# Start of a fused attention and GLU kernel: one reciprocal earlier, half a copy on VectorE, two transposes one group later

## The chip, the cores and the metric

The kernel runs on one core of one Trainium2 chip. The metric is the device time of one execution in microseconds. An execution's span in its profile is about 2 us shorter than its time (228.0 against 229.98 in the profiled run of before).

The profile's single records, one for each instruction, give starts and ends to a nanosecond; they differ by up to 0.005 us from one view to another. A landing is the moment at which a DMA's data has arrived. An eviction is the copy of a finished group of products out of its PSUM tile (q_sb<-q_ps of 128x256 took 0.39 us in the mean in the profile of before).

## The reference, cut to what matters

```python
xn = _layernorm(A_x)                      # 2048 rows of 512, bf16
s  = _A_ref(xn, A_wqkv, A_wo)             # qkv projection, attention over 8 keys with dilation 2, 32 heads of 16
g  = silu(_B_ref(xn, w_gate, w_up, w_down))   # gelu(xn w_gate) * (xn w_up), then w_down
return A_x + s * g
```

## The kernel before

The 2048 rows are 16 tiles of 128 rows. Tiles 0 to 3 form the first block of 512. To start TensorE early, the first q and k projections are done for tiles 0 and 1 alone (256 columns), and later for tiles 2 and 3. Before it has anything to do, TensorE runs products on constants ("warm-up"). Products of 128 columns start 0.107 us apart up to 6.13 us in the profile of before and 0.056 apart from there on. That the warm-up brings this step forward is an assumption.

```python
def first_moments(t):
    nc.vector.bn_stats(out=stats[:, t, :], in_=x_sb[:, t, :])
    nc.vector.bn_aggr(out=mv[:, t, :], in_=stats[:, t, :])
    nc.scalar.activation(out=std[:, t, :], in_=mv[:, t, 1:2], func=AF.Sqrt, bias=epsc[:], scale=1.0)

def first_normalize(t):
    nc.vector.reciprocal(out=rstd[:, t, :], in_=std[:, t, :])
    normalize(t)                       # xn = (x - mean) * rstd, VectorE

def transpose(t, parts=1, copy=None):
    tr = mm.tile([P, NC * P], BF16, name="tr", tag="mm")
    # ... four TensorE transposes into tr, then tr -> xnT in `parts` pieces:
    for k in range(parts):
        c = slice(k * NC // parts, (k + 1) * NC // parts)
        if copy is None:
            nc.scalar.activation(out=dst[:, c], in_=src[:, c], func=AF.Copy)
        else:
            copy(out=dst[:, c], in_=src[:, c])

# ... the start
warm_up(18, TQ // 2); warm_up(4, P)
first_moments(0); first_moments(1)
first_normalize(0); transpose(0)
first_normalize(1); warm_up(4, P)
transpose(1, parts=2); warm_up(4, P)
first_moments(2); first_moments(3)
first_normalize(2); first_normalize(3)
# ... q of tiles 0 and 1: 16 products into q_ps, chunks 0 and 1 of xnT first
for fo in range(NC):
    qkv(0, fo, 0, HQ, qs[fo])          # ScalarE evicts the four q groups
transpose(HT, copy=nc.vector.tensor_copy)              # tile 2
for fo in range(NC, 2 * NC):
    qkv(0, fo, 0, HQ)                  # k groups: 4 products, ScalarE evicts
    if fo == NC:
        transpose(HT + 1, copy=nc.vector.tensor_copy)  # tile 3
```

The warm-up results, the transposes and the k groups all take their PSUM space from one pool, `mm`, of four banks (`mm = pool("mm", 4, space=PSUM)`); q_ps has its own. I call the k groups k0 to k3 and the transposes of tile n tr*n*.

The softmax here doesn't subtract the row's maximum and nothing guards it: scores larger than these inputs give would overflow.

## Time and profile before

| | before |
|---|---|
| time, median of 3 runs | 229.72 us (229.64 to 230.14) |
| span of the profiled execution | 228.0 us |
| TensorE busy | 222.4 us, 98% |
| VectorE busy | 147.6 us, 65% |
| ScalarE busy | 129.8 us, 57%, 213 instructions |
| q_ps starts | 6.88 us |
| TensorE's clock reaches full rate | 6.13 us |

TensorE is busy throughout (98%), so only what delays its products counts. The page's sum says nothing on a change in the first 11 us: for that the chain of work and the timelines of these microseconds are to be read, which the prediction shows. The row on the clock is read from single product records: the starts of 128-column products lie 0.107 us apart before it and 0.056 apart after it.

### The profile page before, as it was taken

Reading aid. Unit: us, or ns where it says so; the run is one execution under the profiler, and the core shown is the slowest. Engines: PE = TensorE matmul, PEld = TensorE weight load, DVE = VectorE, ACT = ScalarE, POOL = GpSimd, SP = SyncE. Lnnn points to the kernel's source line nnn. Section 1 sums busy time; section 2 is a strip of 40 time slices with the busy share of each in tenths; the row PEclk is TensorE's granted clock in tenths of the full one; section 3 lists DMA queues with packets and bytes.
Section 4 is the critical chain, followed back from the end, with each engine's and each line's share of the span. In section 5 each row is a group of like instructions: output and inputs, shape, how many; then the busy total and the mean of one; then the engine's idle time right before and its main releaser. Section 6 shows DMA issues by size and latency. Waiting matters only on the chain.

```text
span 228.0 us, 3495 instructions
## 1 busy us (share of the span) xinstructions
PE 222.4 (98%) x1300; PEld 106.8 (47%) x1320; DVE 147.6 (65%) x234; ACT 129.8 (57%) x213; POOL 12.8 (6%) x44
## 2 busy tenths in 40 slices
PE   8999999999999999999999999999999999999993
PEld 6864444444444444444444444444444444444453
DVE  4585996999496298865945369735476429943324
ACT  3779769774423876467621686746642387647210
POOL 1046023100000000110000000000000000000000
PEclk9999999999999999999999999999999999999999
DMA  6999589971399211110287511110149700001011
GB/s 166 354 372 372 146 169 197 247 202 38 101 195 206 70 25 29 26 29 0 92 169 168 139 30 23 26 35 5 39 119 206 169 27 3 0 6 26 0 45 48
DMA packets 31264, 24.62 MB, mean 108 GB/s; under 512 B 10896, under 2 KB 31248, under 8 KB 31248
## 3 DMA queue, kind: packets, MB, share of 16 engines
q1 hardware_dynamic: 31248, 24.41, 42.8%
q8 instruction: 10, 0.16, 0.3%
q14 instruction: 6, 0.05, 0.1%
HBM read 18.74 MB, written 4.34 MB: 101 GB/s over the span
## 4 chain that ended last, share of the span: by engine, by line
PE 95%; ACT 2%; issue 1%; DVE 0%; ACTq 0%; DVEq 0%
PE u_ps L238 21%; PE y_ps L394 21%; PE g_ps L238 19%; PE qkv_ps L238 17%; PE s_ps L410 6%; PE L_ps L295 3%; PE o_ps L357 3%; PE warm_ps L220 2%; PE q_ps L238 1%; ACT u L384 1%; ACT L382 1%; PE tr L203 1%; PE den_ps L315 0%; ACT xnT L212 0%; ACT ge L382 0%
## 5 line engine op out<-in xcount | busy, mean ns | idle before, releaser
L238 PE MATMUL u_ps<-xnT,wu_sb 128*128 128x512 bf16 x224 | 57.5, 379 | 0.3
L238 PE MATMUL g_ps<-xnT,wg_sb 128*128 128x512 bf16 x213 | 56.3, 379 | 0.4
L394 PE MATMUL y_ps<-wd_sb,h 128*128 128x512 bf16 (+1 forms) x236 | 50.2, 366 | 0.1
L386 DVE TENSOR_TENSOR h<-ge,u 128x512 bf16<-128x512 bf16 x56 | 23.7, 424 | 37.0 <-ACT u L384 36.6
L284 DVE TENSOR_TENSOR pk<-q_sb,k_sb 128x2048 bf16<-128x2048 bf16 x32 | 37.5, 1216 | 7.0 <-ACT k_sb L259 7.0
L382 ACT ACTIVATE ge<-g_ps 128x512 bf16<-128x512 f32 x56 | 33.5, 598 | 14.9 <-PE g_ps L238 13.8
L384 ACT ACTIVATE u<-u_ps 128x512 bf16<-128x512 f32 x56 | 33.5, 598 | 14.7 <-PE u_ps L238 14.7
L238 PE MATMUL qkv_ps<-xnT,wqkv_sb 128*128 128x512 bf16 (+1 forms) x203 | 40.5, 354 | 0.3
L343 DVE TENSOR_TENSOR pv<-E,v_arr 128x2048 bf16<-128x2048 bf16 x32 | 38.6, 1218 | 0.2 <-issue 0.2
L394 PEld LDWEIGHTS <-h 128*128 128x128 bf16 x238 | 23.3, 98 | 25.3
L238 PEld LDWEIGHTS <-wu_sb 128*128 128x128 bf16 x224 | 21.9, 98 | 26.6 <-issue 0.3
L238 PEld LDWEIGHTS <-wg_sb 128*128 128x128 bf16 x224 | 21.3, 98 | 27.3 <-issue 3.0
L402 ACT ACTIVATE sl<-y_ps 128x512 bf16<-128x512 f32 (+1 forms) x17 | 9.7, 572 | 41.4 <-PE y_ps L394 39.0
L238 PEld LDWEIGHTS <-wqkv_sb 128*128 128x128 bf16 x224 | 21.8, 98 | 19.8 <-issue 0.4
L418 DVE TENSOR_TENSOR m<-s_ps,sl 128x512 bf16<-128x512 f32 (+1 forms) x17 | 11.2, 657 | 22.2 <-PE s_ps L410 22.2
L410 PE MATMUL s_ps<-wo_sb,oT 128*128 128x512 bf16 (+1 forms) x66 | 15.8, 366 | 0.2
L262 ACT ACTIVATE vst<-qkv_ps 128x512 bf16<-128x512 f32 x16 | 9.6, 598 | 6.5 <-PE qkv_ps L238 6.5
L188 POOL TENSOR_TENSOR rstd<-rstd,mhalf 128x1 f32<-128x1 f32 x12 | 7.7, 640 | 87.4 <-DVE rstd L185 87.4
L259 ACT ACTIVATE k_sb<-qkv_ps 128x512 bf16<-128x512 f32 (+1 forms) x20 | 10.2, 516 | 3.5 <-PE qkv_ps L238 3.2
L369 DVE TENSOR_TENSOR oT<-o_ps,rb 128x1024 bf16<-128x1024 f32 x8 | 9.4, 1216 | 3.1 <-DMA rb<-rs_d 3.1
L256 ACT ACTIVATE q_sb<-qkv_ps 128x512 bf16<-128x512 f32 (+1 forms) x16 | 8.7, 544 | 3.2 <-PE qkv_ps L238 3.0
L410 PEld LDWEIGHTS <-oT 128*128 128x128 bf16 x68 | 6.7, 98 | 7.2
(46 smaller groups left out, 105.9 us busy)
## 6 DMA issues: line engine op xcount, KB each, us to landing
v_arr<-vT SPq DMA_DIRECT2D x16, 520.0 KB, 5.4
vT<-vst SPq DMA_DIRECT2D x16, 128.0 KB, 1.8
out_dram<-o_t SPq DMA_DIRECT2D x15, 128.0 KB, 1.8
wg_sb<-in_B_w_gate_dram SPq DMA_DIRECT2D x2, 896.0 KB, 10.7
wu_sb<-in_B_w_up_dram SPq DMA_DIRECT2D x2, 896.0 KB, 12.3
wd_sb<-in_B_w_down_dram SPq DMA_DIRECT2D x1, 1792.0 KB, 12.3
wqkv_sb<-in_A_wqkv_dram SPq DMA_DIRECT2D x3, 512.0 KB, 5.2
x_sb<-in_A_x_dram SPq DMA_DIRECT2D x3, 512.0 KB, 11.6
```

The costliest lines, as they stand in the source:

```text
L238: nc.tensor.matmul(ps, lhsT=w[:, dk, lo : lo + P], rhs=xnT[j][:, dk, i0 : i0 + n], start=(dk == 0), stop=(dk == NC - 1),)
L259: nc.scalar.activation(out=k_sb[:, c, lo : lo + n], in_=ps, func=AF.Copy)
L262: nc.scalar.activation(out=vst[:], in_=ps, func=AF.Copy)
L284: nc.vector.tensor_tensor(out=pk[:], in0=st[j]["q"][:], in1=k_sb[:, :, off : off + TQ], op=ALU.mult)
L343: nc.vector.tensor_tensor(out=pv[:], in0=st[j]["E"][:, wh, :].unsqueeze(1).to_broadcast([P, 4, TQ]), in1=st[j]["va"][:, 4 * g : 4 * g + 4, ...
L382: nc.scalar.activation(out=ge[:], in_=g_ps[:], func=AF.Gelu_apprx_tanh)
L384: nc.scalar.activation(out=u[:], in_=u_ps[:], func=AF.Copy)
L386: nc.vector.tensor_tensor(out=h[:], in0=ge[:], in1=u[:], op=ALU.mult)
L394: nc.tensor.matmul(y[:], lhsT=st[j][fc][:, tt * P : (tt + 1) * P], rhs=wd_sb[:, fc, cols], start=(fc == 0), stop=(fc == NF - 1),)
L402: nc.scalar.activation(out=sl[:], in_=y[:], func=AF.Silu)
L410: nc.tensor.matmul(s[:], lhsT=st[j]["oT"][:, g, tt * P : (tt + 1) * P], rhs=wo_sb[:, g, cols], start=(g == 0), stop=(g == NC - 1),)
L418: nc.vector.tensor_tensor(out=m[:], in0=s[:], in1=sl[:], op=ALU.mult)
```

## The change

Three things: the reciprocal of tile 0 is put between the statistics and the aggregate of tile 1, where VectorE waits anyway (0.034 us in the profile of before, 4.362 to 4.396). VectorE copies the first half of tile 1's transpose, where ScalarE copied both halves one after the other (from 6.44 and 6.72 us in before). And the transposes of tiles 2 and 3 come one k group later, since VectorE gets to these tiles later. The intent is to start q_ps earlier.

```diff
+    def first_stats(t):
+        nc.vector.bn_stats(out=stats[:, t, :], in_=x_sb[:, t, :])
     def first_moments(t):
-        nc.vector.bn_stats(out=stats[:, t, :], in_=x_sb[:, t, :])
         nc.vector.bn_aggr(out=mv[:, t, :], in_=stats[:, t, :])
 ...
-    def first_normalize(t):
+    def first_rstd(t):
         nc.vector.reciprocal(out=rstd[:, t, :], in_=std[:, t, :])
-        normalize(t)
 ...
-            if copy is None:
+            if copy is None or k % 2:
                 nc.scalar.activation(out=dst[:, c], in_=src[:, c], func=AF.Copy)
 ...
+    first_stats(0)
     first_moments(0)
+    first_stats(1)
+    first_rstd(0)
     first_moments(1)
-    first_normalize(0)
+    normalize(0)
     transpose(0)
-    first_normalize(1)
+    first_rstd(1)
+    normalize(1)
     warm_up(4, P)
-    transpose(1, parts=2)
+    transpose(1, parts=2, copy=nc.vector.tensor_copy)
     warm_up(4, P)
 ... (tiles 2 and 3: the same calls, split into their parts)
-    transpose(HT, copy=nc.vector.tensor_copy)
     for fo in range(NC, 2 * NC):
         qkv(0, fo, 0, HQ)
-        if fo == NC:
-            transpose(HT + 1, copy=nc.vector.tensor_copy)
+        if fo < NC + 2:
+            transpose(HT + fo - NC, copy=nc.vector.tensor_copy)
```

More of the change, by code (lines that the diff above doesn't have):

```diff
@@ L474 @@
     warm_up(4, P)
+    first_stats(0)
     first_moments(0)
+    first_stats(1)
+    first_rstd(0)
     first_moments(1)
-    first_normalize(0)
+    normalize(0)
     transpose(0)
-    first_normalize(1)
+    first_rstd(1)
+    normalize(1)
     warm_up(4, P)
-    transpose(1, parts=2)
+    transpose(1, parts=2, copy=nc.vector.tensor_copy)
     warm_up(4, P)
-    first_moments(2)
-    first_moments(3)
-    first_normalize(2)
-    first_normalize(3)
+    for t in (2, 3):
+        first_stats(t)
+        first_moments(t)
+    for t in (2, 3):
+        first_rstd(t)
+        normalize(t)
     q4 = att.tile([P, NC, TQ], F32, name="q4_ps", tag="quad")
```

## The prediction

> **What bounds the kernel now.** I read the page's chain of work that ended last first. It is TensorE nearly everywhere, so a microsecond is won or lost only where TensorE issues later or earlier.
>
> ```profile
> PE 95%; ACT 2%; issue 1%; DVE 0%; ACTq 0%; DVEq 0%
> ```
>
> The change touches only the first 11 us, so I read the same chain there in order of time:
>
> ```profile
> 0.84 4.43 PE warm_ps L220 x22
> 5.26 0.47 PE tr L203 x4
> 5.73 0.43 PE warm_ps L220 x4
> 6.16 0.26 PE tr L203 x4
> 6.42 0.02 issue
> 6.44 0.39 ACT xnT L212
> 6.83 0.04 issue
> 6.88 1.91 PE q_ps L238 x16
> 8.79 0.22 PE tr L203 x4
> 9.01 0.44 PE qkv_ps L238 x4
> ```
>
> The columns are start, us, what. Up to 6.42 the path runs through TensorE's own warm-up products, not through VectorE. Then ScalarE's copy of the first half of tile 1's transpose (6.44 to 6.83) holds q_ps, which starts at 6.88. From there TensorE issues without a gap, a 128x256 product each 0.109 us (16 in 1.744 us from 6.882 to 8.627, single records). The waits of TensorE and its weight load over the first 8 us agree: only two matter.
>
> ```profile
> PE q_ps L238 <- ACT xnT L212: 0.2, 1, 0.2
> PEld L238 <- DMA wqkv_sb<-in_A_wqkv_dram: 0.2, 1, 0.2
> ```
>
> The second is the q weights: their last packet lands at 6.607 and the weight load starts at 6.651. So q_ps can't start before about 6.66: at most 0.22 us is to be had. VectorE's timeline of 4 to 7 us, with start and duration:
>
> ```profile
> 4.39 0.18 DVE L173 BATCH_NORM_AGGREGATE mv<-stats 128x2 f32<-128x6 f32 x1
> 4.49 0.13 DVE L179 RECIPROCAL rstd<-std 128x1 f32<-128x1 f32 x1
> 4.66 0.41 DVE L194 TENSOR_SCALAR xn<-x_sb,mv,rstd 128x512 bf16<-128x512 bf16 x1
> 4.99 0.15 DVE L179 RECIPROCAL rstd<-std 128x1 f32<-128x1 f32 x1
> 5.18 0.41 DVE L194 TENSOR_SCALAR xn<-x_sb,mv,rstd 128x512 bf16<-128x512 bf16 x1
> ```
>
> Tile 0's normalize waits 0.17 us for the reciprocal just ahead of it. The rows that decide my prediction are ScalarE's evictions of 8.6 to 11.3 us:
>
> ```profile
> 8.82 1.21 ACT L256 ACTIVATE q_sb<-q_ps 128x256 bf16<-128x256 f32 x4 [0.59 <-PE q_ps L238]
> 9.90 1.50 ACT L259 ACTIVATE k_sb<-qkv_ps 128x256 bf16<-128x256 f32 x4
> ```
>
> All four q evictions wait for the last q_ps product (8.517 + 0.273 = 8.790). They issue 0.27 us apart, so the first k group is evicted only from 9.900 to 10.315, though TensorE finished it at 9.45.
>
> [...]
> - [...]128-column products start 0.107 us apart up to 6.064 and 0.056 apart from 6.134.[...]
> - [...]For the 128x512 bf16 copy[...] the trace has 0.424.[...] ScalarE's half copy took 0.384.
> - [...]
> - [...]Here four buffers rotate, and the change alters which group gets which.
>
> **The change, part by part.**
>
> 1. Reciprocal of tile 0 ahead of tile 1's aggregate. The aggregate must wait for its statistics (ends 4.362, starts 4.396). The reciprocal's input is ready (ScalarE's root ends at 4.179), so it goes into that gap at about 4.28. The normalize then starts about 0.10 after the aggregate, as the reciprocal does now: 4.50 in place of 4.66, ending at 4.91. But TensorE is in warm-up until 4.955 + 0.107 = 5.062, so the transposes of tile 0 move from 5.132 to 5.062, 0.07 and not 0.17. The four then issue 0.107 apart and end their block at 5.49 instead of 5.53 (0.04 won). Four warm-ups and four transposes of tile 1 follow with half of the saving lost if the clock step stays at 6.08: tile 1's transposes end at 6.38 to 6.41 (now 6.190 + 0.219 = 6.409). Gain 0.00 to 0.04, I take 0.025.
>
> 2. Half copy on VectorE. It starts 0.04 after the transposes, 6.42,[...] and q_ps starts 0.05 later: 6.76 in place of 6.88. ScalarE's half, if it waits for VectorE's, ends near 7.14; it is first needed by the ninth product at 6.76 + 0.87 = 7.63. Nothing lost there. Parts 1 and 2 together: 0.12 us gained, q_ps products issued by 8.50 (were 8.627), last one done at 8.67 (was 8.79).
>
> 3. Statistics of tile 2 now sit behind the half copy. The statistics start near 6.65 and those of tile 3 near 7.45 (was 6.994): some 0.42 us later down the line. Tile 2 is normalized by about 8.83 (now 8.40) and tile 3 by 9.34.
>
> 4. Transposes one group later, which part 3 needs. Order before: tr2, k0, tr3, k1, k2, k3. After: k0, tr2, k1, tr3, k2, k3. TensorE's work is the same (group 0.436, four transposes 0.223), and k0's weights land at 8.423, just ahead of 8.50. The buffers are not the same. The pool of four hands them out in turn. Before, k2 takes tr2's buffer, free when VectorE's copy ends at 9.475; k2 starts at 9.947 without waiting, and k3 takes k0's, free at 10.315, with its start at 10.383: 0.07 to spare. (In the records k2's first product waits on VectorE's semaphore and k3's on ScalarE's, which confirms the rotation.) After, k2 is the fourth allocation behind k0 and takes **k0's** buffer. TensorE would be ready for it at 8.50 + 2 x 0.436 + 2 x 0.223 = 9.82. But k0's eviction stands behind four q evictions: they start at 8.70, k0's at 8.70 + 1.07 = 9.77, it ends at 9.77 + 0.415 = 10.19, and the product starts 0.05 later, 10.24. So TensorE waits 0.42 us, a wait that doesn't exist now.
>
> Sum: k2 starts at 10.24 against 9.947: 0.29 us later. That is 0.42 of new wait less 0.12 of earlier start (the same work lies between). The later groups don't wait again: k3 needs tr2's buffer (VectorE has copied it by 9.8), the next q group k1's (evicted by 10.46, wanted at 11.1).
>
> **What becomes of 0.29 us.** After 10 us I looked for waits at a fixed time that could absorb it. The gap between starts of TensorE's products shows single gaps of 0.2 us, half of them missing records, and only one early wait for another engine, 21.01, on ScalarE (eviction of v, table load, gelu). That chain starts when TensorE finishes v, and moves with it. x rows 4 to 7 land at 12.136 and are transposed only at 17.77, with the normalize done at 16.6; the up weights land at 17.43 and are used at 18.85. No load is late, so nothing absorbs the shift: span 228.0 + 0.3, time 229.72 + 0.29 = 230.0.
>
> **The rivals.**
> - A. The change does what its author wants: q_ps 0.12 to 0.2 us earlier and nothing behind it, 229.55. For it: all TensorE work is equal and the wait above is inferred from the order of allocation. Against it: the semaphores in the records fit the rotation at every one of four groups.
> - B. The first part gains nothing (clock step or the 6.607 landing moves): the wait for k0's buffer counts from q_ps's end, so k2 comes at 10.34, 0.39 later, 230.1. For it: the weight load already waits for this DMA.
> - C. VectorE is late: tile 2's normalize ends at 8.9 or more and tile 2's transposes (due 8.94) wait, and ScalarE's q evictions stand behind tile 3's root. For it: only 0.05 to spare. Against it: up to 0.4 us hides under the same wait for k0's buffer. If the root came 0.2 late, 230.2.
> - D. The step of the array's clock comes at another time in other executions: either sign, some tenths, in both kernels alike. It widens the range only.
>
> **Range and chances.** The central sum is +0.29 (+0.13%), 230.0. The rivals span 229.5 to 230.2, and the three runs of before span 0.5 us. So 229.55 to 230.4 should hold it 8 times in 10. 2% is 4.6 us, over ten times any of these terms: faster or slower by over 2% would need a cause outside the first 11 us, 0.5% each.
>
> **What would show it.** Right: q_ps starts near 6.76 behind a VectorE copy of 128x256[...], ScalarE's half after it; tile 0's normalize at 4.50; the third k group starts near 10.24 after a TensorE idle of about 0.4 us, put down to ScalarE's k_sb eviction; from 11 us on all stages 0.2 to 0.4 later. Wrong: no idle at about 9.8 (then the buffers turn otherwise, rival A); q_ps not before 6.85 (B); idle ahead of tile 2's transposes of over 0.4 us (C); stages after 20 us not shifted like those at 11 us (something absorbs it).

One term of the sum goes with them: how long VectorE's half copy takes. With it parts 1 and 2 came to q_ps at 6.76 in place of 6.88, 0.12 us gained, and the sum to k2 at 10.24 against 9.947, +0.29 us, 230.0 in all. The profile of after has 0.291 us for this copy. That ScalarE's half comes after VectorE's was an assumption (in the profile of after it starts at 6.376, VectorE's ends at 6.342).

## The result, and the profile after

The changed kernel took 230.02 us (median of 6, 229.78 to 230.32), the kernel before 229.73 us in the same rounds (median of 6). The ratio is 1.0012, 95% interval 0.9999 to 1.0024: the same within 2%. The predicted number, 230.0, is met almost exactly. The profile shows at once that it isn't met for the predicted reason.

First the chain of work after, in order of time (start, us, what):

```profile
2.18 4.31 DMA wqkv_sb<-in_A_wqkv_dram
6.49 0.04 issue
6.54 1.92 PE q_ps L239 x16
8.46 0.56 PE qkv_ps L239 x4
9.02 0.22 PE tr L204 x4
9.24 0.44 PE qkv_ps L239 x4
9.68 0.22 PE tr L204 x4
9.90 7.85 PE qkv_ps L239 x56
```

q_ps starts at 6.54, not at the predicted 6.76 nor at the old 6.88, and what releases it is the landing of the q weights, no longer ScalarE's copy. k0 takes 0.56 in place of 0.44, because the k weights land at 8.37 and hold it for 0.11 us. And from the transposes of tile 3 on TensorE runs through: the predicted wait of 0.42 us ahead of k2 isn't there. (This chain counts a step from the modelled end of the one before, hence 9.90; by the single records k2's first product starts at 9.76.)

VectorE's timeline after shows that part 1 did on VectorE what was predicted, and that the half copy takes 0.29 us:

```profile
4.29 0.14 DVE L181 RECIPROCAL rstd<-std 128x1 f32<-128x1 f32 x1
4.41 0.18 DVE L175 BATCH_NORM_AGGREGATE mv<-stats 128x2 f32<-128x6 f32 x1
4.50 0.38 DVE L195 TENSOR_SCALAR xn<-x_sb,mv,rstd 128x512 bf16<-128x512 bf16 x1
4.95 0.16 DVE L181 RECIPROCAL rstd<-std 128x1 f32<-128x1 f32 x1
5.15 0.41 DVE L195 TENSOR_SCALAR xn<-x_sb,mv,rstd 128x512 bf16<-128x512 bf16 x1
6.05 0.29 DVE L215 COPY xnT<-tr 128x256 bf16<-128x256 bf16 x1 [0.49 <-PE tr L204]
```

Tile 0's normalize is at 4.50 (4.66 before), but tile 1's only at 5.15 (5.18): 0.16 us for the first, 0.03 for the second.

ScalarE's evictions keep their shape. k0 is still evicted only behind the four q evictions, but nobody waits for it:

```profile
8.50 1.21 ACT L257 ACTIVATE q_sb<-q_ps 128x256 bf16<-128x256 f32 x4 [0.21 <-PE q_ps L239]
9.57 1.64 ACT L260 ACTIVATE k_sb<-qkv_ps 128x256 bf16<-128x256 f32 x4
```

Two things must be kept apart before the traces are compared. The clock's step to full rate fell at 3.70 us in this execution and at 6.13 us in the profiled one of before. Between the two times 128-column products start 0.056 us apart here and 0.107 apart there. The step also moves without the change: two profiles of the kernel before have it at 6.13 and 5.34. So the 0.34 us by which q_ps is earlier here can't be credited to it, and neither can the 0.14 us by which the span is shorter (227.86 against 228.0). And a longer median time goes with a shorter span in the one profile. That asked for more executions of both kernels and for each part by itself.

**Theories before the experiments.** A: the buffers turn otherwise than predicted, nothing is lost, the early part gains 0.05 to 0.2 us, and the +0.29 us between the medians is scatter. B: a loss of some 0.3 us is real, and the first profile hid it behind its early clock step. C to G came up on the way and are stated where they were tested.

The built programs say which PSUM bank each tile got, so the first part of A can be looked up (tiles in the order of the program, with the number of the bank):

```
            tr2  k0   tr3  k1   k2         k3         q0 (tiles 2,3)  q1
before       1    2    3    0    1 (tr2's)  2 (k0's)   3 (tr3's)       0 (k1's)
            k0   tr2  k1   tr3  k2         k3         q0              q1
after        1    2    3    0    2 (tr2's)  1 (k0's)   3 (k1's)        0 (tr3's)
```

The pool isn't a ring. In the changed kernel k2 takes tr2's bank, which VectorE's copy frees early (at 9.70 us in the profile of after), and not k0's. With k0 in bank 1 and k2 in bank 2 the predicted wait can't come about.

### The profile page after: what moved, and what is told of

It is laid out like the page before. It is cut to its first block, busy times and chain, and to the rows that moved or that the text cites. A ratio compares the mean times of both kernels' runs of the same rounds, so it can differ in the third digit from the quotient of the medians.

```text
span 227.9 us, 3516 instructions
## 1 busy us (share of the span) xinstructions
PE 222.8 (98%) x1320; PEld 106.0 (47%) x1320; DVE 147.8 (65%) x235; ACT 129.6 (57%) x212; POOL 12.8 (6%) x44
## 4 chain that ended last, share of the span: by engine, by line
PE 94%; DMA 2%; ACT 1%; SPq 1%; DVE 0%; issue 0%; DVEq 0%
PE y_ps L395 21%; PE u_ps L239 21%; PE g_ps L239 21%; PE qkv_ps L239 18%; PE s_ps L411 6%; PE L_ps L296 3%; PE o_ps L358 3%; DMA wqkv_sb<-in_A_wqkv_dram 2%; PE q_ps L239 1%; ACT L383 1%; SPq L85 1%; PE den_ps L316 0%; ACT ge L383 0%; ACT vst L263 0%; ACT xnT L213 0%; PE tr L204 0%
## 5 line engine op out<-in xcount | busy, mean ns | idle before, releaser
L239 PE MATMUL g_ps<-xnT,wg_sb 128*128 128x512 bf16 x224 | 57.6, 379 | 0.0
```

The costliest lines, as they stand in the source:

```text
L239: nc.tensor.matmul(ps, lhsT=w[:, dk, lo : lo + P], rhs=xnT[j][:, dk, i0 : i0 + n], start=(dk == 0), stop=(dk == NC - 1),)
```

## The experiments

All outputs are right. One table first; "us" are medians of six runs, except that before has eleven:

| run | edit | us | before, same rounds | ratio, 95% interval |
|---|---|---|---|---|
| after_again | the changed kernel | 230.09 | 230.01 | 1.0000 (0.9984 to 1.0016) |
| before_again | the kernel before | 229.91 | 230.01 | 0.9991 (0.9974 to 1.0008) |
| shared_buffer | changed, k2 forced into k0's bank | 230.66 | 230.01 | 1.0025 (1.0007 to 1.0043) |
| no_shift | changed, transposes in their old place | 230.50 | 230.01 | 1.0018 (1.0001 to 1.0035) |
| recip_only | before, reciprocal alone | 229.88 | 229.95 | 0.9986 (0.9970 to 1.0002) |
| half_only | before, half copy alone | 230.02 | 229.95 | 0.9999 (0.9983 to 1.0014) |
| shift_only | before, later transposes alone | 229.88 | 229.95 | 0.9991 (0.9976 to 1.0007) |
| early_weights | changed, q and k weights loaded earlier | 230.60 | 229.95 | 1.0026 (1.0008 to 1.0043) |
| absorbed_wait | changed, ScalarE's wait taken earlier | 230.16 | 230.08 | 0.9999 (0.9978 to 1.0019) |
| absorbed_q_first | the same, q weights earlier | 230.66 | 230.08 | 1.0016 (0.9999 to 1.0034) |
| recip_again | recip_only once more | 229.94 | 230.08 | 0.9990 (0.9975 to 1.0006) |
| absorbed_padded | absorbed_wait, one idle ScalarE instruction | 230.14 | 229.80 | 1.0019 (1.0005 to 1.0033) |

The intervals are 0.13% to 0.2% wide to either side, 0.3 to 0.45 us. The terms in question are 0.02 to 0.4 us. So most verdicts rest on the single records of the traces, which repeat to some nanoseconds:

| run | clock step | x rows of tile 0 landed to tile 0's, tile 1's normalize | end of tr1 to q_ps | k2 after q_ps | first gate product to end of span |
|---|---|---|---|---|---|
| before | 6.13 | 1.812, 2.332 | 0.473 | 3.065 | 210.010 |
| before_again | 5.34 | 1.812, 2.333 | 0.472 | 3.064 | 209.996 |
| recip_again | 3.72 | 1.647, 2.290 | 0.472 | 3.078 | 210.014 |
| shift_only | 5.42 | (row landing late) | 0.473 | 3.082 | 209.997 |
| half_only | 4.38 | 1.813, 2.334 | 0.475 | 3.346 | 210.051 |
| after | 3.70 | 1.644, 2.288 | 0.525 (q weights late) | 3.218 | 210.055 |
| after_again | 3.77 | 1.643, 2.288 | 0.474 | 3.082 | 210.062 |
| no_shift | 4.38 | 1.650, 2.293 | 0.476 | 3.931 | 210.051 |
| shared_buffer | 5.14 | 1.645, 2.291 | 0.476 | 3.483 | 210.041 |
| early_weights | 6.20 | 1.645, 2.287 | 0.475 | 3.648 | 210.061 |
| absorbed_wait | 6.42 | 1.645, 2.287 | 0.379 | 3.917 | 210.058 |
| absorbed_q_first | 4.60 | 1.643, 2.288 | 0.381 | 3.254 | 210.049 |
| absorbed_padded | 6.93 | 1.645, 2.350 | 0.383 | 3.081 | 210.010 |

All are microseconds. "After q_ps" counts from q_ps's first product to k2's.

### after_again and before_again

No edit.

> The changed kernel once more, unedited, to see whether +0.29 us is real and where the step of the array's clock falls. Theory A (the third k group takes another buffer than predicted, nothing is lost, the early part gains 0.05 to 0.2 us, and +0.29 us of the medians is scatter): ratio 0.9990 to 1.0005; third k group starts 9.7 to 9.85 us. Theory B (a loss of about 0.3 us is real and the first profile happened to hide it behind an early clock step at 3.6 us): ratio 1.0008 to 1.0020, and with a clock step near 6 us a TensorE wait of 0.2 us or more between 8 and 11 us.

> The kernel before, unedited: what two sets of runs of one and the same program differ by. Ratio 1.0000, within 0.0008 either way, under both theories. If its clock step comes earlier than the 6.08 us of the first profile, q_ps starts at 6.60 to 6.70 in place of 6.88 (then the q weights' landing holds it); if it comes again near 6 us, 6.85 to 6.9.

The ratio of the changed kernel is 1.0000 this time; that of the unchanged kernel to itself is 0.9991. The kernel before had medians of 229.73, 230.01, 229.95, 230.08 and 229.80 us in five sessions, and the changed kernel 230.02 and 230.09. So +0.29 us is no more than what sessions of one kernel differ by (0.35 us; they ran on at least three chips). Within the rounds of one session the fairer measure is the ratio: 1.0012 the first time, 1.0000 the second, and 0.9991 for a kernel against itself. In after_again's profile k2 starts at 9.65 us, just before the 9.7 to 9.85 that was expected for theory A; the clock step had come at 3.77. Its first profile wasn't a lucky one that hid a loss, since the second shows no wait of 0.2 us between 8 and 11 us either. Theory B falls as far as a loss of 0.3 us goes; the interval of after_again leaves 0.16%, 0.37 us, to either side, and the sign of the difference stays open by times alone.

Before_again had its clock step at 5.34 us, and q_ps started at 6.66 in place of 6.88 with the same program. That is more than the change can do. The expected 6.60 to 6.70 came, but not for the reason given: the q weights had landed at 6.35, and ScalarE's copy still held q_ps.

### shared_buffer: the predicted wait made on purpose

```diff
+    kps = mm.tile([P, HQ], F32, name="qkv_ps", tag="mm")[:]
     for fo in range(NC, 2 * NC):
-        qkv(0, fo, 0, HQ)
+        if fo in (NC, NC + 2):                      # k0 and k2 share one tile
+            project(kps, wqkv_sb, fo * P, 0, 0, HQ)
+            qkv(0, fo, 0, HQ, kps)
+        else:
+            qkv(0, fo, 0, HQ)
```

> The changed kernel with the third k group forced into the first k group's buffer, as the prediction had supposed. Theory A: here, and not in the changed kernel, TensorE waits 0.28 to 0.42 us for ScalarE's eviction of the first k group, and the third k group starts about 10.0 to 10.25 us; ratio to the kernel before 1.0004 to 1.0016, and 1.0012 to 1.0018 times that of the changed kernel. Theory B with the buffer as the cause: the same time as the changed kernel within 0.0005.

From TensorE's and ScalarE's timelines of 8 to 12 us of this run:

```profile
9.46 0.39 PE L204 MATMUL tr<-ident,xn 128*128 128x128 bf16 x4
10.10 2.13 PE L239 MATMUL qkv_ps<-xnT,wqkv_sb 128*128 128x256 bf16 x18 [0.26 <-ACT k_sb L260]
```

```profile
8.56 1.21 ACT L257 ACTIVATE q_sb<-q_ps 128x256 bf16<-128x256 f32 x4
9.64 0.69 ACT L260 ACTIVATE k_sb<-qkv_ps 128x256 bf16<-128x256 f32 x2
```

k2 starts at 10.108, 0.419 us later than TensorE could issue it. (The 0.26 in the line is less, because the profile counts idle from the modelled end of the product before, not from its issue.) The prediction's sum for this wait was 0.42. So its arithmetic was right for a kernel in which k2 has k0's bank, and the changed kernel isn't that kernel. The median is 0.57 us above after_again of the same rounds, more than the wait; the ratio of 1.0025 lies above the expected 1.0004 to 1.0016, which its interval takes in down to 1.0007.

### recip_only and recip_again: part 1 alone

```diff
+    first_stats(0)
     first_moments(0)
+    first_stats(1)
+    first_rstd(0)
     first_moments(1)
-    first_normalize(0)
+    normalize(0)
```

> The kernel before with the reciprocal of tile 0 put ahead of tile 1's aggregate, and nothing else. Tile 0's normalize starts at 4.50 in place of 4.66. Theory A: gain 0.00 to 0.05 us at q_ps with a late clock step, up to 0.15 us with an early one, the q weights' landing (6.5 to 6.65) setting the floor; ratio 0.9993 to 1.0003. Theory B with this part as the cause: 1.0008 or more.

> The reciprocal alone once more, since the profile of its first run fell in an execution of 1343 us. Against the kernel before, counted from the landing of tile 0's rows: tile 0's normalize starts 0.16 to 0.2 us earlier, tile 1's at most 0.05 us earlier, since it waits for ScalarE's root of tile 1 and that is no earlier; so q_ps 0.0 to 0.05 us earlier. Ratio 0.9985 to 1.0007. Rival (the whole 0.17 us arrives): q_ps 0.15 us earlier.

The profiled execution of recip_only took 1343.46 us. TensorE was slow from its first to its last product; the page's lines for the span and for one tile say it:

```profile
span 1341.7 us, 3515 instructions
...
L395 PE MATMUL y_ps<-wd_sb,h 128*128 128x512 bf16 (+1 forms) x238 | 300.9, 1628 | 0.0
```

The mean of such a product was 1628 ns against 366 in the page of before, while its other five runs took 229.58 to 229.91 us. It tells nothing on the change, and the kernel was run once more.

In recip_again tile 0's normalize starts 1.647 us after its rows have landed, against 1.812: 0.165 us earlier, as predicted. Tile 1's starts 0.043 us earlier (2.290 against 2.333), and this is what q_ps hangs on. The chain is: aggregate of tile 1, root on ScalarE, reciprocal, normalize. VectorE's timelines, first before_again, then recip_again:

```profile
4.53 0.18 DVE L173 BATCH_NORM_AGGREGATE mv<-stats 128x2 f32<-128x6 f32 x1
4.62 0.13 DVE L179 RECIPROCAL rstd<-std 128x1 f32<-128x1 f32 x1
4.79 0.41 DVE L194 TENSOR_SCALAR xn<-x_sb,mv,rstd 128x512 bf16<-128x512 bf16 x1
5.12 0.16 DVE L179 RECIPROCAL rstd<-std 128x1 f32<-128x1 f32 x1
```

```profile
4.45 0.18 DVE L175 BATCH_NORM_AGGREGATE mv<-stats 128x2 f32<-128x6 f32 x1
4.55 0.38 DVE L195 TENSOR_SCALAR xn<-x_sb,mv,rstd 128x512 bf16<-128x512 bf16 x1
4.99 0.16 DVE L181 RECIPROCAL rstd<-std 128x1 f32<-128x1 f32 x1
```

In the first, the second reciprocal starts 0.33 us after the normalize. In the second the same 0.33 would put it at 4.88 (an estimate), but it waits for ScalarE's root, which ends at 4.961 in the single records, 0.51 us after the aggregate's start, as in the profile of before (4.39 to 4.90). So of 0.165 us 0.043 is left. The times of both runs lie below 1 (0.9986 and 0.9990), both with intervals that hold 1.

### half_only: part 2 alone

```diff
-            if copy is None:
+            if copy is None or k % 2:
 ...
-    transpose(1, parts=2)
+    transpose(1, parts=2, copy=nc.vector.tensor_copy)
```

> The kernel before with half of tile 1's copy on VectorE, and nothing else. VectorE's half takes 0.29 us in place of ScalarE's 0.38; here it stands in program order ahead of tile 2's statistics, so tile 2's normalize moves from 8.4 to about 8.8 and TensorE waits for it at 8.5 (transposes in their old place). Theory A: q_ps 0.1 us earlier, then a wait of 0.1 to 0.4 us at tile 2's transposes; ratio 0.9998 to 1.0012. Theory B with this part as the cause: 1.0010 or more.

The expected wait came: 0.27 us at tile 2's transposes, which VectorE's later statistics hold up (k2 comes 3.346 us after q_ps in place of 3.065). The expected gain didn't come at all: from the end of tr1 to q_ps it is 0.475 us, and 0.472 or 0.473 where ScalarE copies both halves. VectorE's copy is 0.093 us shorter (0.291 against 0.384), and q_ps starts 0.146 us after its end where it starts 0.051 after ScalarE's. The gain is used up to the last few nanoseconds. VectorE's and TensorE's lines:

```profile
6.16 0.29 DVE L214 COPY xnT<-tr 128x256 bf16<-128x256 bf16 x1 [0.49 <-PE tr L203]
```

```profile
6.59 0.60 PE L238 MATMUL q_ps<-xnT,wqkv_sb 128*128 128x256 bf16 x4 [0.24 <-DMA wqkv_sb<-in_A_wqkv_dram]
```

The DMA named in the second had landed at 6.49; the next run shows what held q_ps.

### absorbed_wait: why the half copy gains nothing

In the changed kernel the first q product has to wait for two engines: for ScalarE's copy of tile 0 and for VectorE's half of tile 1. In the built program ScalarE's wait is on the product, the DMA's on the weight load ahead of it, and VectorE's is an instruction of its own ahead of that load. Theory D is that this second wait, not VectorE, costs the time: the weight load can't be done ahead any more. The edit lets the last warm-up product read tile 0's copy, so that TensorE has waited for ScalarE by then (the helper got an argument for it):

```diff
-    warm_up(4, P)
+    warm_up(4, P, last=xnT[0][:, 0, 0:P])     # rhs of the last of the four products
```

> The changed kernel, where the last warm-up product reads tile 0's transposed copy, so that TensorE has waited for ScalarE before it comes to q_ps and has only VectorE left to wait for. Theory D (in the changed kernel VectorE's copy is 0.093 us shorter, 0.291 against 0.384, but q_ps starts 0.146 us after its end in place of 0.051, because the second wait sits on the weight load as a separate instruction; so the half copy gains nothing): from the end of VectorE's copy to q_ps 0.05 us, and from the end of tile 1's transposes to q_ps 0.38 us in place of 0.47, unless the q weights land later than that. Rival E (VectorE's writes are seen later than ScalarE's whatever waits): still 0.14 and 0.47 us. Time: at most 0.1 us less than the changed kernel, ratio to before 0.9988 to 1.0008, not to be told from it.

From the end of VectorE's copy to q_ps it is now 0.052 us, and from the end of tr1 0.379 (and 0.381 and 0.383 in the two kernels built on this one), against 0.472 to 0.476 in nine of the ten others; the tenth is the first profile of after, where the weights came late. Theory D holds, rival E falls. TensorE's weight loads, first in after_again, then in this run:

```profile
6.53 0.56 PEld L239 LDWEIGHTS <-wqkv_sb 128*128 128x128 bf16 x6 [0.39 <-DMA wqkv_sb<-in_A_wqkv_dram]
```

```profile
6.53 0.10 PEld L240 LDWEIGHTS <-wqkv_sb 128*128 128x128 bf16 x1
6.90 0.10 PEld L240 LDWEIGHTS <-wqkv_sb 128*128 128x128 bf16 x1 [0.27 <-issue]
```

In after_again the first load comes at 6.533, after VectorE's copy (ended 6.418), the separate wait (6.458 to 6.509) and just ahead of q_ps (6.564). So of the 0.146 us the separate wait takes 0.091, the load starts 0.024 later, and the product 0.031 after that. The profile puts this idle time down to the DMA, whose last packet landed at 6.258, long before: a wait for several things is given to one of them, and here it is the wrong one. In absorbed_wait the load is done at 6.53 while VectorE's copy runs from 6.56 to 6.85, and q_ps follows at 6.904.

The time is no better (ratio 0.9999), and the profiled execution was a long one of 230.65 us: the k weights landed at 9.43 us instead of 8.1 to 8.4, and k0 waited 0.83 us for them.

### shift_only and no_shift: part 3 alone and the rest without it

```diff
 shift_only, from before; no_shift is the reverse edit of the changed kernel
-    transpose(HT, copy=nc.vector.tensor_copy)
     for fo in range(NC, 2 * NC):
         qkv(0, fo, 0, HQ)
-        if fo == NC:
-            transpose(HT + 1, copy=nc.vector.tensor_copy)
+        if fo < NC + 2:
+            transpose(HT + fo - NC, copy=nc.vector.tensor_copy)
```

> The kernel before with the transposes of tiles 2 and 3 one group later, and nothing else. Theory A: no TensorE wait comes or goes, third k group within 0.05 us of 9.95 (late clock step); ratio 0.9995 to 1.0005. Theory B with this part as the cause (k weights at 8.4 or buffers): 1.0008 or more.

> The changed kernel with the transposes of tiles 2 and 3 back in their old place (ahead of the first and behind the first k group). Tile 2's normalize ends near 8.5 to 8.85 us and the transposes are wanted at 8.3 to 8.5. Theory A: TensorE waits 0.05 to 0.4 us for VectorE at tile 2's transposes; ratio 0.9998 to 1.0015, 0.0003 to 0.0015 above the changed kernel. Theory B with the later place as the cause of the loss: faster than the changed kernel by 0.0008 or more.

Alone, the shift costs 0.017 us: k2 comes 3.082 us after q_ps instead of 3.065, held for a moment by VectorE's copy of tr2, whose bank it takes. Nothing else changes.

Without it, the changed kernel waits. In the weight loads of 8 to 11 us of no_shift:

```profile
8.56 0.23 PEld L204 LDWEIGHTS <-xn 128*128 128x128 bf16 x4 [0.39 <-DVE xn L195]
9.36 0.33 PEld L239 LDWEIGHTS <-wqkv_sb 128*128 128x128 bf16 x4 [0.57 <-DMA wqkv_sb<-in_A_wqkv_dram]
```

The first is the expected wait for tile 2's normalize (0.28 us of lost issue by the single records). The second is bad luck: the k weights landed at 9.32 us in this execution. The median, 230.50 us, is 0.41 above after_again of the same rounds, and all six of its runs are above all six of the changed kernel's. So the shift is what makes the half copy harmless: the trace shows 0.28 us of wait without it and 0.017 with it, while how much of the median's 0.41 is due to late weights isn't known. It doesn't gain anything by itself.

### early_weights and absorbed_q_first: is it the weights?

In the first profile of after, the q and k weights hold q_ps and k0. Two kernels load them earlier:

```diff
 early_weights, from the changed kernel: rows 0, 1, q weights, rows 2, k weights, rows 3
-    for t in range(TPQ - 1):
+    for t in range(TPQ // 2):
         load_x(t)
     load_w(wqkv_sb, A_wqkv, 0, D)
-    load_x(TPQ - 1)
-    for i in range(1, 3):
-        load_w(wqkv_sb, A_wqkv, i * D, (i + 1) * D)
+    load_x(TPQ // 2)
+    load_w(wqkv_sb, A_wqkv, D, 2 * D)
+    load_x(TPQ - 1)
+    load_w(wqkv_sb, A_wqkv, 2 * D, 3 * D)
 absorbed_q_first, from absorbed_wait: rows 0, 1, q weights, rows 2, rows 3, k weights
```

> The changed kernel with the q weights loaded ahead of tile 2's rows and the k weights ahead of tile 3's. If the landings of the weights are what is left to hold the start (6.5 us for q, 8.4 us for k in the profile of after), q lands near 6.1 and k near 8.0, q_ps starts at 6.1 (early clock step) to 6.75 (late), and the kernel is 0.1 to 0.4 us faster than the changed one: 0.9983 to 0.9996 of it. Rival: rows of tiles 2 and 3 land up to 0.4 and 0.7 us later, VectorE's normalizes end after 9.0 us, and TensorE waits at tile 2's transposes what it gained: within 0.0004 of the changed kernel.

> The same with the q weights loaded ahead of tile 2's rows alone, k weights and tile 3's rows in their old order. q weights land near 5.9 us, tile 2's rows near 6.3, tile 3's near 6.65, so q_ps is held by VectorE's copy alone and starts at 6.35 to 6.5 with an early clock step, about 6.8 with a late one; no new wait at tile 2's transposes, unlike the run with both weights moved. Then the k weights' landing near 8.2 holds the first k group. Expected ratio to before 0.9980 to 1.0002. Rival: VectorE waits for tile 2's rows and passes it on; then a TensorE wait of over 0.1 us at tile 2's transposes.

Early_weights is slower than the kernel before (ratio 1.0026, 230.60 us). The changed kernel wasn't in these rounds, so against it only the traces count. The rival, a wait at tile 2's transposes, came, and more strongly than written. The clock step was late (6.20), and q_ps started at 6.90, after the 6.1 to 6.75 that were expected. q weights landed at 5.93 and k weights at 7.80, but tile 3's rows only at 8.15. VectorE takes the statistics of tile 3 ahead of tile 2's normalize, so both normalizes are late (9.16 and 9.68 us), and TensorE stands still ahead of tr2:

```profile
9.63 0.40 PE L205 MATMUL tr<-ident,xn 128*128 128x128 bf16 x4 [0.39 <-DVE xn L196]
```

That is 0.56 us of issue, more than there was to gain.

In absorbed_q_first q_ps started at 6.456, the earliest of all, and there is no wait at tr2. But then k0 waited 0.16 us for the k weights, which landed at 8.315. The time was not better (230.66 us, ratio 1.0016; one slow run of 233.37). So in this execution, with the transposes shifted, the landing of the k weights was the floor: q_ps's 1.74 us ended before it. In the order of before, four transposes lie between and cover 0.22 us of it.

### absorbed_padded: a pause of ScalarE that goes with the count of instructions

From the first gate product to the end of the span, the four kernels without the half copy take 209.996 to 210.014 us, and all eight with the half copy and no padding take 210.041 to 210.062. That is 0.045 us, far from the change's place. The single records show it at 39 us, where in after_again TensorE waits 0.06 us for an eviction; behind it is a later eviction of u at 34 us. ScalarE's timeline of before_again, then of after_again:

```profile
33.99 0.60 ACT L384 ACTIVATE u<-u_ps 128x512 bf16<-128x512 f32 x1 [0.32 <-PE u_ps L238]
34.60 1.28 ACT L290 ACT_TABLE_LOAD   x1
```

```profile
34.22 0.60 ACT L385 ACTIVATE u<-u_ps 128x512 bf16<-128x512 f32 x1 [0.64 <-PE u_ps L239]
34.84 1.28 ACT L291 ACT_TABLE_LOAD   x1
```

In the second, the eviction starts 0.36 us after its wait for TensorE had been met, in the first 0.04: a pause of 0.31. (The second pause that the expectation below names, near 36 us, is none of its own: there ScalarE follows its table load, which the first has put off.) The kernels with the half copy have 212 ScalarE instructions, the others 213. Theory F is that the place of such a pause follows the number of instructions ahead of it. The edit adds one idle instruction at 2.4 us to absorbed_wait:

```diff
     nc.scalar.activation(out=std[:, 0, :], in_=epsc[:], func=AF.Sqrt, bias=epsc[:], scale=1.0)
+    nc.scalar.activation(out=std[:, 1, :], in_=epsc[:], func=AF.Sqrt, bias=epsc[:], scale=1.0)
```

> The kernel with the absorbed wait, plus one idle 128x1 root on ScalarE at 2.1 to 2.4 us, where ScalarE has nothing to do. Every kernel with the half copy has one ScalarE instruction fewer (212 against 213) and takes 210.04 to 210.06 us from the first gate product to the end; every kernel without it 210.00 to 210.01. In the former ScalarE pauses 0.34 and 0.31 us at two fixed instructions near 34 and 36 us, and TensorE loses 0.05 us to it at 39 us. Theory F (the place of the pause follows the number of instructions ahead of it, not the copy itself): with 213 instructions again, 210.00 to 210.02 us from the first gate product to the end and no pause at the eviction of u near 34 us. Rival G (the copy on VectorE shifts something else): still 210.04 to 210.06. q_ps 0.05 us behind VectorE's copy as in the absorbed run; the clock's step and the k weights' landing may hide it in the time: ratio to before 0.998 to 1.001.

With 213 instructions the pause is gone from this place, and from the first gate product to the end it is 210.010 us, though the half copy is still there:

```profile
34.27 0.60 ACT L387 ACTIVATE u<-u_ps 128x512 bf16<-128x512 f32 x1 [0.33 <-PE u_ps L241]
34.89 1.28 ACT L293 ACT_TABLE_LOAD   x1
```

G falls, and F holds as far as one profile with one more instruction can show: the pause goes with the count. That it moves to another place is not shown; after 25 us no idle time of ScalarE grew by over 0.15 us in this run against before_again. What ScalarE does in the pause no run shows. The added instruction had a price of its own: it writes to the place of tile 1's root, so the real root got a separate wait ahead of it, and tile 1's normalize came 0.06 us later (2.350 in the table against 2.287 in absorbed_wait).

The first full-rate product of this execution came latest of all, at 6.93 us. The ratio is 1.0019 with an interval wholly above 1, although this kernel has both the absorbed wait and no pause; why it isn't faster stays open. No version here beats the kernel before beyond the scatter.

## Why the prediction was right or wrong, point by point

The number, the range and the verdict were right, and the mechanism was wrong, so the number was met by luck. Two steps failed, and they failed in opposite directions.

- **"After, k2 is the fourth allocation behind k0 and takes k0's buffer" (part 4): wrong.** The program gives k2 tr2's bank. The inference rested on "the pool of four hands them out in turn", and the confirmation by semaphores was none: in before, k2's wait for VectorE and k3's for ScalarE fit any order that gives k2 the bank of tr2 and k3 that of k0, and the later waits for VectorE fit the data as well as the bank. The 0.42 us of that wait was sized right (0.419 in shared_buffer), for a kernel that wasn't the one to be predicted. This is the step that carried +0.42 of the sum; 0.017 us came in its place.
- **"q_ps starts 0.05 later" than VectorE's copy (part 2): wrong.** It was 0.146. The copy took 0.291, and ScalarE's half followed it (start 6.452, VectorE's end 6.418 in after_again), as had been assumed. But the product now has two engines to wait for, and the second wait keeps the weight load from being done ahead (it came at 6.533 in after_again, behind the end of VectorE's copy at 6.418). Part 2 gained 0.00 in place of 0.09 us. absorbed_wait shows the cause.
- **Part 1: right on VectorE; what reaches TensorE depends on the clock step.** Tile 0's normalize at 4.50 came as written. The prediction had the warm-up products hold back tile 0's transposes and took 0.025 us. With an early step it was tile 1's chain through ScalarE that bound, and 0.043 came through.
- **Part 3: right in kind, nearly in size.** Counted from the landing of tile 0's rows, tile 2's normalize starts at 5.18 us in after_again and at 4.79 in before_again, 0.39 later where 0.42 was predicted. No_shift shows that the shift is needed. (Without the half copy tile 3's statistics start when its rows land, 6.97 us in before and 6.75 in before_again, so the difference isn't the same in every pair of profiles.)
- **"Nothing absorbs the shift": right**, as far as it can be: from the first gate product on, all kernels take the same time to 0.02 us, but for ScalarE's pause of 0.045, which nothing in the profile of before could have told.
- **Rival A** (nothing behind it) is what came of the buffers, without its gain. **Rival B** (the first part gains nothing) is near the truth, 0.043 us in place of 0.12, but the q weights held q_ps by 0.05 us in the first profile only. **Rival C** (VectorE late at tile 2's transposes) didn't come in the changed kernel: in after_again the normalize ends at 8.53 and the transposes start at 8.74 without a wait. **Rival D**, the clock, was underrated: it was put at some tenths in both kernels alike, and with the k weights' landing it is the largest term in the start (q_ps at 6.88 and 6.66 in two executions of the kernel before).

The sum in place of the predicted one, by the single records, is: 0.043 us gained by the reciprocal, 0.00 by the half copy, 0.017 lost at k2 and 0.045 at ScalarE's pause, with at times 0.1 us at the k weights. That is a loss of 0.02 to 0.12 us. Whether it is +0.1 or 0 in the time no run resolves, and the +0.29 us that made the number come out can't be told from scatter: the same comparison gave a ratio of 1.0000 the second time.

## What to carry to other kernels

Look up which buffer each tile got in the built program before you predict a wait for one: a pool of four need not be a ring, and a semaphore's engine can fit several stories. When a product's inputs come from two engines, count the extra wait: it can also keep the weight load from being done ahead (q_ps started 0.146 us after the later engine's end here, and 0.052 with one of the waits taken earlier), so let an earlier product take one of the two waits. And a change of a few hundredths of a microsecond is judged by intervals between single records of several executions, not by one trace against another with its clock step at another time (3.70 to 6.93 us here), and not by medians.

## What else the traces show

- The clock's step to full rate comes at no fixed time. In 13 profiles the first full-rate start lay at 3.70 to 6.93 us of the span, with the first product at 0.84: 2.9 to 6.1 us after it, a spread of 3.2. The traces' clock records put the step at 3.59 to 6.67, and show full rate for 221.87 or 225.28 us in every one of the 13. What sets the time of the step no run here shows.
- One execution was slow from end to end: 1341.7 us, 14 products of 512 columns in 18.43 us, 1.316 us each against 0.216, while the granted clock printed with it is 1.0. Its trace holds no clock record at all, so that 1.0 says nothing, and what slowed TensorE stays open.
- A product with two engines to wait for (q_ps in half_only and after_again) started 0.146 us after the later one's end, against 0.051 with one, since the separate wait stood ahead of the weight load.
- ScalarE has a pause that goes with its number of instructions: 0.31 us at the eviction of u in the profiles with 212 instructions, none there in those with 213; TensorE lost 0.045 us to it.
- The landing of one load scatters. The k weights (512 KB) landed at 9.32 and 9.43 us in two profiles, at 8.07 to 8.42 in the others with this order of loads, though they were issued at 3.21 us in the late ones and in before alike. In the traces a load's landing is counted in 16 steps of a semaphore: in no_shift 15 of them had come by 8.15 us and the last at 9.32. TensorE waited 0.57 and 0.83 us for it.
